# A fused attention and MLP kernel: one DMA per output tile, score pairs placed by estimated queues, the last tile in three pieces, and a new order of the first batch

## Chip, cores and metric

The kernel runs on one core of a Trainium2 chip. The metric is the device time of one execution in microseconds (us). The profile comes from one separate, profiled execution.

## What is computed

For each of 8 batches: attention over 12 heads of 448 tokens with 64 features, then a mixer of rank 32 over the tokens, then an MLP with 768 to 3072 to 768 features, both with a residual.

```python
q_n, k_n = rmsnorm(q, g_q), rmsnorm(k, g_k)            # q, k, v: (8, 12, 448, 64) float32
attn = softmax(q_n @ k_n^T / sqrt(64))
x = (attn @ v), heads side by side                     # (8, 448, 768)
u = x + (x^T @ U @ V)^T                                # U (448, 32), V (32, 448): over the tokens
out = u + relu(u @ w_ch1) @ w_ch2                      # (768, 3072), (3072, 768); float32
```

## The kernel before

**Tiles.** Matmuls are in bf16. The 448 tokens of a batch stand as three and a half windows of 128; the half window (column SM = 384) is shared by two consecutive batches, which share the tiles uT (u transposed, the input of the MLP) and hT (its hidden layer). Four heads are a *group*, a group has two *pairs* of heads, a batch has three groups and six pairs. Score and product blocks are in PSUM tiles from two pools (`ps_sc`, two tiles of two banks, and `ps`, four of one bank); E (the exps of a pair) has two buffers, x three, the output tile ob three.

**One group's way.** SP loads q, k and v (`load_qk` L92, `load_v` L105). `squares` (L135) on ACT or POOL and `sums` (L161, two DVE reductions of 128x896) give the sums of squares, `roots` (L165, two small ACT instructions) the factors, `scale` (L173) the normed q and k, `values` (L199) the bf16 copy of v. In groups 0 to 5, PE transposes q and k (`turn` L349; `take_q` and `take_k`, L357 and L366, copy them from PSUM on DVE); from group 6 on, SP issues transposing DMAs (`turn_dma`, L375 to L381) and POOL multiplies the gains in (`take_dma`, L386).

**Attention.** In the first batches scores are made by `Sc` (L403: block r of a pair, exp at L416 on ACT), later by `Spair` (L421), which makes all seven score matmul groups of a pair and their exps in one go: its matmuls are at L427, L436 and L438. `V(pair, half)` (L450) multiplies E with the values (matmuls L462 and L466) and normalizes on DVE (L469, L470) into x.

**Mixer.** In the first batch `mix_t0` (L496) makes a piece of tz = x^T U, and `mix` (L506) adds V's product to x's transpose and writes uT. Later batches use `mix_t` (L480: 24 matmuls, the DVE copy tb at L487), `mix_tr` (L489: two transposes of tb, a DVE copy tT) and `mix_rows` (L526: eight pieces; matmul L537, the residual on DVE at L542, a transposing DMA to uT at L548).

**MLP.** `up(b, ht)` (L550) makes one of 24 row blocks of the hidden layer (6 matmuls of 448 columns at L554, relu on ACT at L561 or on DVE); `down` (L579) makes a half (384 columns) of an output tile in four quarters of 6 matmuls (L586), adds u on DVE (L596), and issues two DMAs per tile, one of 64 partitions each (L604). `w1` and `w2` are loaded in chunks by POOL (`weights`).

**What sets the order.** The engines execute in the order in which the program issues, and each engine's queue is in order. Ahead of the loop the first group is made by hand. The first batch's attention follows the table `extra` (L632 to L656): what is issued behind score block (pair, r), with `keep_busy` (L237: blocks of 4 small matmuls that write nothing that is used). Everything else is in two lists, `att` (attention of batches 1 to 7) and `mlp` (mixer and MLP). The loop at L854 merges them: by their estimated costs it takes an attention item when `due` says so and `ready` (L845) allows it, else an MLP item. `at` holds an estimated end of the queue of PE, ACT and DVE, which `runs(engine, us)` advances in the functions. `ready` lets a pair (`Spair`) start except directly behind a mixer item:

```python
if f is Spair:
    return im == 0 or not mixes(mlp[im - 1][1])
```

Of the kernel before, what the change touches and what calls it, by code (L numbers as in the profile page):

```python
# [9 lines left out]
FP32 = mybir.dt.float32  # L10
# [3 lines left out]
ALU = AluOpType  # L14
# [12 lines left out]
def kernel(  # L27
# [13 lines left out]
    nc = tc.nc  # L41
# [75 lines left out]
    def stage_tiles(gi):  # L117
        staged[gi] = [stage.tile([P, NM + 2, D], FP32, name=nm, tag=nm) for nm in ("qf", "kf", "vf")]
        ssqs[gi] = normp.tile([P, 2, NM + 2], FP32, name="ssq", tag="ssq")
        normed[gi] = [normp.tile([P, NT, 2, D], BF16, name="qn", tag="qn", bufs=1)]  # L120
        if gi < DMA_FROM:
            normed[gi].append(kp[:, :NT].rearrange("p j (c d) -> p j c d", c=2))
        else:
            normed[gi].append(kp)
        normed[gi] += [va_bufs[gi % 3], vl_bufs[gi % 3]]
# [73 lines left out]
    def values(gi):  # L199
        tv, va, vl = staged[gi][2], *normed[gi][2:]  # L200
        nc.gpsimd.tensor_copy(va[:, :, :D], tv[:, :NM, :])
        for e in range(2):
            nc.gpsimd.tensor_copy(vl[e * R:(e + 1) * R, :, e * D1:e * D1 + D], tv[e * R:(e + 1) * R, NM:, :])
# [93 lines left out]
    Urows = moe_U.rearrange("(p j) r -> p j r", j=NT)  # L297

    def load_u():
        for i in range(2):  # L300
            nc.sync.dma_start(Uf[i * R:(i + 1) * R, :NJ, :], Urows[:, i * NJ:(i + 1) * NJ, :])
        nc.sync.dma_start(Uf[R:P, NJ, :], Urows[:, 2 * NJ, :])
        nc.sync.dma_start(Uf[0:R, NJ + 1, :], Urows[:, 2 * NJ, :])
        nc.sync.dma_start(Vf, moe_V.rearrange("(m r) s -> m r s", m=1).to_broadcast([NQ, rank, S]))
# [175 lines left out]
    def mix_t(b):  # L480

        pt = ps.tile([P, KD, rank], FP32, name="pu", tag="ps")
        for dt in range(KD):
            for j in range(NW):
                nc.tensor.matmul(pt[:, dt, :], xs[b][:, j, dt * P:(dt + 1) * P], Ub[:, j if j < NJ else NJ + b % 2, :],  # L485
                                 start=(j == 0), stop=(j == NW - 1))
        nc.vector.tensor_copy(tb_bufs[b % 2][:, :KD * rank], pt.rearrange("p k r -> p (k r)"))  # L487

    def mix_tr(b):  # L489
        pt = ps.tile([P, 2, P], BF16, name="pw", tag="ps")  # L490
        for i in range(2):
            nc.tensor.transpose(pt[:, i, :], tb_bufs[b % 2][:, i * P:(i + 1) * P], ident)
        tTs[b] = headp.tile([P, 2, P], BF16, name="tT", tag="tT")
        nc.vector.tensor_copy(tTs[b], pt)

    def mix_t0(lo, hi, scalar=False):  # L496

# [78 lines left out]

    down_ps, down_sb = {}, {}

    def down(b, col, half, part, nparts):  # L579
        key = (b, col, half)  # L580
        if part == 0:
            down_ps[key] = ps.tile([P, HALF], FP32, name="po", tag="ps")
        po = down_ps[key]
        n = KH // nparts
        for ht in range(part * n, (part + 1) * n):
            nc.tensor.matmul(po, hT[:, ht, col:col + P], w2b[:, ht, half * HALF:(half + 1) * HALF],  # L586
                             start=(ht == 0), stop=(ht == KH - 1))
        runs("pe", 0.98)
        if part < nparts - 1:
            return  # L590
        runs("dve", 0.55)
        h = slice(half * HALF, (half + 1) * HALF)
        if half == 0 or b == 0:
            down_sb[(b, col)] = outp.tile([P, dm], FP32, name="ob", tag="ob")
        ob = down_sb[(b, col)]
        nc.vector.tensor_tensor(ob[:, h], po, urows(b, col, half), ALU.add)  # L596
        if half == 1 or b == 0:
            h = h if b == 0 else slice(0, dm)

            def rows(b, j):  # L600
                return out[b].rearrange("(p j) d -> j p d", j=NT)[j]
            for i in range(2):
                o = rows(b, i * NJ + col // P) if col != SM else rows(b - i, 2 * NJ)
                nc.sync.dma_start(o[:, h], ob[i * R:(i + 1) * R, h])  # L604


    pairs = [(b, pr) for b in range(B) for pr in range(NPAIR)]
# [13 lines left out]
    def V2(i, half):  # L621
        return (0.55, V, (*pairs[i], half))

    pool = nc.gpsimd

    def scales(gi):
        return [(0, roots, (gi,)), (0, scale, (gi, 0, pool)), (0, scale, (gi, 1, pool))]

    def turns(gi):
        return [(0.4, turn, (gi, 0)), (0, take_q, (gi, 0)), (0, take_q, (gi, 1)), (0.4, turn, (gi, 1)), (0, take_k, (gi, 0))]  # L630

    extra = {  # L632
        (0, 0): [(0, keep_busy, (8,))],
        (0, 1): [(0, keep_busy, (8,))],
        (0, 2): scales(1) + [(0, squares, (2, 1, pool)), (0, keep_busy, (8,))],
        (0, 3): [(0, keep_busy, (8,))],
        (1, 0): [(0, keep_busy, (8,))],
        (1, 1): [V2(0, 0), (0, keep_busy, (6,))],
        (1, 2): [(0.4, turn, (1, 0)), (0, take_q, (1, 0)), (0, take_q, (1, 1)), (0, keep_busy, (8,))],
        (1, 3): [(0.4, turn, (1, 1)), (0, take_k, (1, 0)), V2(0, 1), (0, take_k, (1, 1)), (0, sums, (2, 1)),  # L640
                 (0, values, (1,)), (0, load, (4,)), (0, weights, (1,))],
        (2, 1): scales(2) + [(0, weights, (1,)), V2(1, 0)],
        (2, 2): [(0, keep_busy, (6,))],
        (2, 3): [V2(1, 1), (0, prep_u, ())],
        (3, 0): [(0, keep_busy, (6,))],
        (3, 1): [V2(2, 0)],
        (3, 2): turns(2),
        (3, 3): [V2(2, 1), (0, take_k, (2, 1)), (0, squares, (3, 0, pool)), (0, values, (2,)), (0, load, (5,)),
                 (0, weights, (1,)), (0, prep_v, (0, 1)), (0, squares, (3, 1, pool)), (0, weights, (1,))],
        (4, 0): [V2(3, 0)],  # L650
        (4, 1): [V2(3, 1), (0, sums, (3, 0))],
        (5, 0): [(0.9, mix_t0, (0, 512))],
        (5, 1): [V2(4, 0)],
        (5, 2): [V2(4, 1), (0.39, mix, (0, 0))],
        (5, 3): [(0.39, mix, (0, 1)), (0.2, mix_t0, (512, 640)), (0, prep_v, (1, NQ)), (0, weights, (2,))],
    }  # L656
    for i in range(NPAIR):
        for r in range(4):
            add_att(0.38, Sc, *pairs[i], r)
            att.extend(extra.get((i, r), []))  # L660
    att.extend([V2(5, 0), V2(5, 1), (0, sums, (3, 1)), (0.39, mix, (0, 2, True)), (0.39, mix, (0, 3, True)), (0.57, up_part, (0, 0, 0, 3)),
                (0.2, mix_t0, (640, dm)), (0.39, mix, (0, 4, True)), (0, roots, (3,)), (0.57, up_part, (0, 1, 0, 3)),
                (0.39, mix, (0, 5)), (0.19, up_part, (0, 0, 3, 4)), (0.19, up_part, (0, 1, 3, 4))])
    first_done = len(att)

# [87 lines left out]
    for b in range(B):  # L753
        for ht in range(KH):
            mlp.append((0.38, up_part, (b, ht, 4, KD), b) if b == 0 and ht < 2 else (1.14, up, (b, ht), b))
            if b < ROWS_FROM and ht % 2 == 0 and ht < 4 * NW:
                mlp.append((0.17, mix_rows, (b, ht // 4, ht // 2 % 2), b))
        cols = (64, 192, 320) if b % 2 == 0 else (384, 0, 128, 256)
        n = len(cols) * 8
        nb = b + 1  # L760
        pre = {}
        if ROWS_FROM <= nb < B:
            pre[n - PRE[nb > 1]] = [(0.77, mix_t, (nb,), nb)]
            pre[n - PRE[nb > 1] + 1] = [(0.11, mix_tr, (nb,), nb)]
            for piece in range(2 * NW):
                pre.setdefault(n - PRE[nb > 1] + 2 + (piece if nb > 1 else piece // 2), []).append(
                    (0.17, mix_rows, (nb, *divmod(piece, 2)), nb))
        tiles = [(col, half) for col in cols for half in range(2)]
        if b == 0:
            tiles.sort(key=lambda t: t[1])  # L770
        for c, (col, half) in enumerate(tiles):
            for part in range(4):
                mlp.extend(pre.get(c * 4 + part, []))
                mlp.append((0.98, down, (b, col, half, part, 4), b))

    a_, b_ = PARTS
    squares_part(0, *a_)
# [13 lines left out]
    for part in PARTS:  # L791
# [3 lines left out]
    fill_mixer()  # L795
    squares(2, 0, nc.gpsimd,
            uT.rearrange("p k c -> p (k c)")[:, :4 * NT * D].bitcast(FP32).rearrange("p (j d) -> p j d", d=D))
    values(0)
    turn(0, 0)
    keep_busy(14)  # L800
    take_q(0, 0, True)
# [5 lines left out]
    sums(1, 1)  # L807
    take_k(0, 1)
    sums(2, 0)
    stage_tiles(3)  # L810
    load_u()
    load_v(2)
    load_qk(3, 0)
    load_qk(3, 1)
    load_v(3)

    ia = im = 0
    ca = cm = 0.0
# [23 lines left out]
    def mixes(f):  # L842
        return f in (mix_t, mix_tr, mix_rows)

    def ready(f, a):  # L845
        if f is Spair:
            return im == 0 or not mixes(mlp[im - 1][1])
        if ca >= a_one:
            return True
        if f is V:  # L850
            return exp_done[a[:2]] <= at["pe"] + 0.1
        return f is not Srows or at["act"] <= at["pe"] + 0.6
# [69 lines left out]
```

## Time and profile before

| | us |
|---|---|
| median of 3 runs | 586.98 (586.29 to 587.7) |
| the profiled execution, its own time | 586.64 |
| its span, first to last instruction | 584.8 |
| PE busy / ACT / POOL / DVE | 572.2 / 307.9 / 210.3 / 196.8 |
| mean granted PE clock | 0.999 of full speed |

The span is what the profile sees, and the profiled execution's own time includes 1.84 us around it. A row such as `L596 DVE TENSOR_TENSOR ob<-po,x 128x384 f32<-128x384 f32 x1` names the line, engine, operation, the tile written and those read, and the shapes; brackets hold the idle time before it and what ended that. A row of PE's waits gives what PE waited for, in us in total, times, and the longest. By the view of windows PE is busy 17.4 of the first 20.0 us, 18.8 of the next 21.3, 276.2 of the 278.7 us up to 320, 259.9 of the 260 up to 580, and none of the last 4.8 us.

### The profile page before, as it was taken

The page shows a single profiled execution, that of the slowest core. Times are in us where ns is not written, and L with a number is a line of the kernel's source. Part 1 is how long each engine was busy: PE and PEld are TensorE (multiplying, and loading weights), DVE is VectorE, ACT ScalarE, POOL GpSimd, SP SyncE. Part 2 cuts the span into 40 slices and gives each one's busy share as a digit, 9 for nine tenths or more (in the row PEclk, how much of TensorE's full clock was granted, in tenths as well). Part 3 has the DMA queues.
Part 4 walks back from the last instruction along what each step waited for, and adds up shares of the span by engine and source line. Part 5 has one row for each costly group of instructions (what it writes and reads, how often), then busy time and mean ns, then how long its engine had stood idle before and what let it go on. Part 6 is the DMA issues. An engine that isn't in the chain of part 4 may idle for free.

```text
span 584.8 us, 11725 instructions
## 1 busy us (share of the span) xinstructions
PE 572.2 (98%) x4826; PEld 338.2 (58%) x4826; DVE 196.8 (34%) x458; ACT 307.9 (53%) x510; POOL 210.3 (36%) x310
## 2 busy tenths in 40 slices
PE   8899999999999999999999999999999999999996
PEld 7555556555665555655556555665556655655563
DVE  6676656212352232521235231442034310410011
ACT  7866661677445776277653578457753344014200
POOL 5995684265314515334523433441531000000000
PEclk9999999999999999999999999999999999999999
DMA  8899999683546642585246735375204210420022
GB/s 229 170 241 241 244 233 231 119 220 52 133 78 167 153 106 35 139 212 130 36 122 109 180 104 123 66 172 149 35 25 92 48 28 1 68 61 1 1 54 55
DMA packets 104509, 68.21 MB, mean 117 GB/s; under 512 B 66568, under 2 KB 101256, under 8 KB 104456
## 3 DMA queue, kind: packets, MB, share of 16 engines
q1 hardware_dynamic: 95044, 58.03, 42.6%
q0 software_dynamic: 9408, 9.44, 9.6%
q8 instruction: 38, 0.62, 0.4%
q14 instruction: 15, 0.12, 0.1%
q10 hardware_dynamic: 4, 0.00, 0.0%
HBM read 52.20 MB, written 11.01 MB: 108 GB/s over the span
## 4 chain that ended last, share of the span: by engine, by line
PE 91%; DMA 3%; DVE 2%; POOL 1%; ACT 1%; issue 1%; SPq 1%; POOLq 0%; ACTq 0%
PE ph L554 36%; PE po L586 36%; PE pv L466 6%; PE sc L436 2%; PE sl L427 2%; PE sl L438 2%; PE pv L462 2%; PE pm L537 2%; DMA qf<-in_q_dram 1%; PE sc L415 1%; ACT E L416 1%; DMA vf<-in_v_dram 1%; DVE ssq L162 1%; DMA qT<-qn 1%; PE pu L485 1%
## 5 line engine op out<-in xcount | busy, mean ns | idle before, releaser
L586 PE MATMUL po<-w2b,hT 128*128 128x384 bf16 x1344 | 237.4, 326 | 0.0
L554 PE MATMUL ph<-uT,w1b 128*128 128x448 bf16 x1140 | 228.7, 352 | 0.0
L586 PEld LDWEIGHTS <-hT 128*128 128x128 bf16 x1344 | 126.8, 98 | 75.5 <-issue 0.6
L554 PEld LDWEIGHTS <-w1b 128*128 128x128 bf16 x1140 | 108.3, 98 | 93.8 <-issue 0.7
L561 ACT ACTIVATE hT<-ph 128x448 bf16<-128x448 f32 x184 | 98.0, 550 | 120.2 <-PE ph L554 118.9
L429 ACT ACTIVATE E<-sl,gg 128x448 bf16<-128x448 f32 x72 | 41.5, 629 | 75.9 <-PE sl L427 75.9
L386 POOL TENSOR_SCALAR qT<-qT,gg 128x448 bf16<-128x448 bf16 x36 | 50.5, 1402 | 81.6 <-DMA qT<-qn 65.2
L193 POOL TENSOR_TENSOR qn<-qf,rs 128x384 bf16<-128x384 f32 x36 | 29.9, 829 | 132.4 <-ACT rs L170 127.5
L469 DVE RECIPROCAL r<-pv 128x4 f32<-128x4 f32 x96 | 17.4, 182 | 167.8 <-PE pv L466 167.6
L441 ACT ACTIVATE E<-sc,gg 128x896 bf16<-128x896 f32 x72 | 69.0, 1022 | 0.0
L596 DVE TENSOR_TENSOR ob<-po,x 128x384 f32<-128x384 f32 x48 | 26.7, 557 | 103.8 <-PE po L586 103.4
L466 PE MATMUL pv<-va,E 128*128 128x65 bf16 x1152 | 57.1, 194 | 0.0
L466 PEld LDWEIGHTS <-E 128*128 128x128 bf16 x1152 | 50.5, 98 | 6.3
L162 DVE TENSOR_REDUCE ssq<-sq 128x14 f32<-128x896 f32 x45 | 46.8, 1078 | 2.4 <-ACT sq L140 2.3
L462 PE MATMUL pv<-vl,E 128*128 128x130 bf16 x192 | 42.2, 220 | 0.3 <-ACT E L416 0.2
L470 DVE TENSOR_TENSOR x<-pv,r 128x256 bf16<-128x256 f32 x96 | 40.7, 424 | 3.3
L416 ACT ACTIVATE E<-sc,gg 128x896 bf16<-128x896 f32 (+1 forms) x42 | 37.5, 950 | 4.1 <-PE sc L415 4.1
L542 DVE TENSOR_TENSOR x<-pm,x 128x384 bf16<-128x384 f32 x48 | 26.2, 552 | 16.5 <-PE pm L537 14.2
L193 POOL TENSOR_TENSOR kp<-kf,rs 128x384 bf16<-128x384 f32 x36 | 29.8, 828 | 0.0
L169 ACT ACTIVATE rs<-ssq,eps 128x28 f32<-128x28 f32 (+1 forms) x25 | 7.8, 314 | 33.4 <-DVE ssq L162 29.2
L462 PEld LDWEIGHTS <-E 128*128 128x128 bf16 x192 | 18.7, 97 | 9.7 <-issue 2.0
L439 ACT ACTIVATE E<-sl,gg 128x448 bf16<-128x448 f32 x36 | 22.9, 637 | 0.0
(102 smaller groups left out, 387.9 us busy)
## 6 DMA issues: line engine op xcount, KB each, us to landing
qf<-in_q_dram SPq DMA_DIRECT2D x23, 448.0 KB, 3.7
kf<-in_k_dram SPq DMA_DIRECT2D x23, 448.0 KB, 6.4
out_dram<-ob SPq DMA_DIRECT2D x50, 192.0 KB, 2.8
vf<-in_v_dram SPq DMA_DIRECT2D x48, 192.0 KB, 5.9
w1b<-in_moe_w_ch_dram POOLq DMA_DIRECT2D x4, 1152.0 KB, 19.8
w2b<-in_moe_w_ch_dram POOLq DMA_DIRECT2D x8, 576.0 KB, 17.7
vf<-in_v_dram SPq DMA_DIRECT2D x48, 32.0 KB, 5.7
out_dram<-ob SPq DMA_DIRECT2D x12, 96.0 KB, 3.6
```

The costliest lines, as they stand in the source:

```text
L162: nc.vector.tensor_reduce(ssqs[gi][:, i, :], sqs.pop((gi, i)), AX, ALU.add)
L193: nc.gpsimd.tensor_tensor(main.rearrange("p (t i) d -> p i t d", i=2), src[:, c, :2 * NJ].rearrange("p (i t) d -> p i t d", i=2), rs[:, c, ...
L386: nc.gpsimd.tensor_scalar(qT[:, a], qT[:, a], gg[:, 0:1], None, ALU.mult)
L416: nc.scalar.activation(es[(b, pr)][:, 2 * r:2 * r + n, :], sc[:, :n, :S], AF.Exp, scale=scal, bias=bias)
L429: nc.scalar.activation(E[:, 4 + i, :], ts[i], AF.Exp, scale=scal, bias=bias)
L441: nc.scalar.activation(E[:, 2 * r:2 * r + 2, :], tiles[r][:, :, :S], AF.Exp, scale=scal, bias=bias)
L462: nc.tensor.matmul(pv[:, i].rearrange("p e d -> p (e d)"), E[:, 2 * NJ, w:w + P], vl[:, lp, :], start=True, stop=False)
L466: nc.tensor.matmul(pv[:, i, e, :], E[:, 2 * j + e, w:w + P], va[:, (first_h + step * e) * NJ + j, :], start=False, stop=(e == 1 and j == N ...
L470: nc.vector.tensor_tensor(xs[b].rearrange("p i (h d) -> p i h d", d=D)[:, 2 * half:2 * half + 2, h0:h0 + step + 1:step, :], pv[:, :, :, :D ...
L554: nc.tensor.matmul(ph, w1b[:, dt, ht * P:(ht + 1) * P], uT[:, dt, off:off + S], start=(dt == 0), stop=(dt == KD - 1))
L561: nc.scalar.activation(hT[:, ht, off:off + S], ph, AF.Relu)
L586: nc.tensor.matmul(po, hT[:, ht, col:col + P], w2b[:, ht, half * HALF:(half + 1) * HALF], start=(ht == 0), stop=(ht == KH - 1))
```

## The change

One. The stores: a new function `store` issues one DMA for an output tile, with an access pattern over both token halves; the tile of column SM keeps two, as its halves belong to two batches. The first two of U's loads become one.

Two. `mix_t` and `mix_tr` now advance the estimated queues of PE and DVE, and a pair may start only where the estimated queues of DVE and ACT are not too far ahead of PE's.

Three. The last output tile (batch 7, column 256) is made in pieces of 384, 256 and 128 columns by `down_end`, each with an add and a DMA of its own.

Four. The first batch: group 1 is scaled behind score block (0, 1) instead of (0, 2); the cast of group 0's values follows it on POOL; SP's loads for group 3 go ahead of U, V and the values (`front_loads`); the products V of pair 0 move behind block (2, 0); group 1's turns go one block earlier; group 2 is scaled behind (2, 2) instead of (2, 1); `prep_u` follows values(2); the mixer's first product, 512 columns at once behind (5, 0), becomes two of 256 behind (5, 0) and (5, 2), and `mix(0, 0)` moves to (5, 3).

```diff
     def load_u():
-        for i in range(2):
-            nc.sync.dma_start(Uf[i * R:(i + 1) * R, :NJ, :], Urows[:, i * NJ:(i + 1) * NJ, :])
+        nc.sync.dma_start(Uf[:, :NJ, :], Urows[:, :2 * NJ, :].rearrange("p (i j) r -> i p j r", i=2))
...
         nc.vector.tensor_copy(tb_bufs[b % 2][:, :KD * rank], pt.rearrange("p k r -> p (k r)"))
+        runs("pe", 0.62)
+        runs("dve", 0.35)
...
         nc.vector.tensor_copy(tTs[b], pt)
+        runs("pe", 0.11)
+        runs("dve", 0.3)
...
+    def store(b, col, h, ob):
+        def rows(b):
+            return out[b].rearrange("(p j) d -> j p d", j=NT)
+        if col == SM:
+            for i in range(2):
+                nc.sync.dma_start(rows(b - i)[2 * NJ, :, h], ob[i * R:(i + 1) * R, h])
+        else:
+            nc.sync.dma_start(rows(b)[col // P:col // P + NJ + 1:NJ, :, h], ob[:, h])
+
+    ENDS = (HALF, 5 * P, dm)
+
+    def down_end(b, col, piece):
+        lo, hi = (0, HALF) if piece == 0 else ENDS[piece - 1:piece + 1]
+        if piece == 0:
+            down_sb[(b, col)] = outp.tile([P, dm], FP32, name="ob", tag="ob")
+        ob = down_sb[(b, col)]
+        po = ps.tile([P, HALF], FP32, name="po", tag="ps")[:, :hi - lo]
+        for ht in range(KH):
+            nc.tensor.matmul(po, hT[:, ht, col:col + P], w2b[:, ht, lo:hi], start=(ht == 0), stop=(ht == KH - 1))
+        nc.vector.tensor_tensor(ob[:, lo:hi], po, xs[b][:, col // P, lo:hi], ALU.add)
+        store(b, col, slice(lo, hi), ob)
...
-            def rows(b, j):
-                return out[b].rearrange("(p j) d -> j p d", j=NT)[j]
-            for i in range(2):
-                o = rows(b, i * NJ + col // P) if col != SM else rows(b - i, 2 * NJ)
-                nc.sync.dma_start(o[:, h], ob[i * R:(i + 1) * R, h])
+            store(b, col, h, ob)
...
+    def front_loads():
+        stage_tiles(3)
+        load_qk(3, 0)
+        load_qk(3, 1)
+        load_u()
+        load_v(2)
+        load_v(3)
...
         (0, 0): [(0, keep_busy, (8,))],
-        (0, 1): [(0, keep_busy, (8,))],
-        (0, 2): scales(1) + [(0, squares, (2, 1, pool)), (0, keep_busy, (8,))],
+        (0, 1): scales(1) + [(0, values, (0,)), (0, front_loads, ()), (0, squares, (2, 1, pool)), (0, weights, (1,)),
+                             (0, keep_busy, (8,))],
+        (0, 2): [(0, keep_busy, (8,))],
...
-        (1, 1): [V2(0, 0), (0, keep_busy, (6,))],
-        (1, 2): [(0.4, turn, (1, 0)), (0, take_q, (1, 0)), (0, take_q, (1, 1)), (0, keep_busy, (8,))],
-        (1, 3): [(0.4, turn, (1, 1)), (0, take_k, (1, 0)), V2(0, 1), (0, take_k, (1, 1)), (0, sums, (2, 1)),
-                 (0, values, (1,)), (0, load, (4,)), (0, weights, (1,))],
-        (2, 1): scales(2) + [(0, weights, (1,)), V2(1, 0)],
-        (2, 2): [(0, keep_busy, (6,))],
-        (2, 3): [V2(1, 1), (0, prep_u, ())],
+        (1, 1): [(0.4, turn, (1, 0)), (0, take_q, (1, 0)), (0, take_q, (1, 1)), (0, keep_busy, (6,))],
+        (1, 2): [(0, keep_busy, (8,))],
+        (1, 3): [(0.4, turn, (1, 1)), (0, take_k, (1, 0)), (0, keep_busy, (4,))],
+        (2, 0): [V2(0, 0), V2(0, 1), (0, sums, (2, 1)), (0, take_k, (1, 1)), (0, values, (1,)), (0, load, (4,))],
+        (2, 1): [V2(1, 0)],
+        (2, 2): scales(2) + [(0, weights, (1,)), (0, keep_busy, (6,))],
+        (2, 3): [V2(1, 1), (0, squares, (3, 0, pool))],
...
-        (3, 2): turns(2),
-        (3, 3): [V2(2, 1), (0, take_k, (2, 1)), (0, squares, (3, 0, pool)), (0, values, (2,)), (0, load, (5,)),
-                 (0, weights, (1,)), (0, prep_v, (0, 1)), (0, squares, (3, 1, pool)), (0, weights, (1,))],
+        (3, 2): [(0.4, turn, (2, 0)), (0, take_q, (2, 0)), (0, take_q, (2, 1))],
+        (3, 3): [(0.4, turn, (2, 1)), (0, take_k, (2, 0)), V2(2, 1), (0, take_k, (2, 1)), (0, values, (2,)), (0, load, (5,)),
+                 (0, prep_u, ()), (0, weights, (1,)), (0, prep_v, (0, 1)), (0, squares, (3, 1, pool)), (0, weights, (1,))],
...
-        (5, 0): [(0.9, mix_t0, (0, 512))],
+        (5, 0): [(0.45, mix_t0, (0, 256))],
         (5, 1): [V2(4, 0)],
-        (5, 2): [V2(4, 1), (0.39, mix, (0, 0))],
-        (5, 3): [(0.39, mix, (0, 1)), (0.2, mix_t0, (512, 640)), (0, prep_v, (1, NQ)), (0, weights, (2,))],
+        (5, 2): [V2(4, 1), (0.45, mix_t0, (256, 512))],
+        (5, 3): [(0.39, mix, (0, 0)), (0.39, mix, (0, 1)), (0.2, mix_t0, (512, 640)), (0, prep_v, (1, NQ)), (0, weights, (2,))],
...
-    values(0)
...
-    stage_tiles(3)
-    load_u()
-    load_v(2)
-    load_qk(3, 0)
-    load_qk(3, 1)
-    load_v(3)
...
         if f is Spair:
-            return im == 0 or not mixes(mlp[im - 1][1])
+            if im > 0 and mixes(mlp[im - 1][1]):
+                return False
+            return at["dve"] <= at["pe"] + 0.3 and at["act"] <= at["pe"] + 1.0
```

In the last batch the `mlp` list drops the two halves of the last tile and gets three `down_end` items of 3.9, 2.6 and 1.3 us of estimated cost instead. `sums(3, 1)` moves behind `mix_t0(640, 768)`.

More of the change, by code (lines that the diff above doesn't have):

```diff
@@ L660 @@
             att.extend(extra.get((i, r), []))
-    att.extend([V2(5, 0), V2(5, 1), (0, sums, (3, 1)), (0.39, mix, (0, 2, True)), (0.39, mix, (0, 3, True)), (0.57, up_part, (0, 0, 0, 3)),
-                (0.2, mix_t0, (640, dm)), (0.39, mix, (0, 4, True)), (0, roots, (3,)), (0.57, up_part, (0, 1, 0, 3)),
+    att.extend([V2(5, 0), V2(5, 1), (0.39, mix, (0, 2, True)), (0.39, mix, (0, 3, True)), (0.57, up_part, (0, 0, 0, 3)),
+                (0.2, mix_t0, (640, dm)), (0, sums, (3, 1)), (0.39, mix, (0, 4, True)), (0, roots, (3,)), (0.57, up_part, (0, 1, 0, 3)),
                 (0.39, mix, (0, 5)), (0.19, up_part, (0, 0, 3, 4)), (0.19, up_part, (0, 1, 3, 4))])
@@ L770 @@
             tiles.sort(key=lambda t: t[1])
+        if b == B - 1:
+            tiles = tiles[:-2]
         for c, (col, half) in enumerate(tiles):
@@ L774 @@
                 mlp.append((0.98, down, (b, col, half, part, 4), b))
+    mlp.extend((3.9 * w, down_end, (B - 1, cols[-1], piece), B - 1) for piece, w in enumerate((1.0, 0.67, 0.34)))
     a_, b_ = PARTS
```

## Prediction

> **What bounds the kernel now.** I read the page's busy times first.
>
> ```profile
> PE 572.2 (98%) x4826; PEld 338.2 (58%) x4826; DVE 196.8 (34%) x458; ACT 307.9 (53%) x510; POOL 210.3 (36%) x310
> PEclk9999999999999999999999999999999999999999
> ```
>
> PE is busy 572 of 584.8 us at full clock, so only PE's idle time, the head and the tail can give anything: nothing in the change shortens a matmul stream. Next the list of PE's waits (line waited for: us in total, times, longest):
>
> ```profile
> PE sc L415 <- ACT E L416: 2.1, 4, 0.9
> ...
> PE sl L427 <- POOL qT L386: 1.1, 1, 1.1
> PE sl L438 <- DVE tb L487: 0.6, 1, 0.6
> PE sl L427 <- DVE x L542: 0.5, 1, 0.5
> PE sc L415 <- DVE kT L369: 0.5, 1, 0.5
> ```
>
> The rows with L427 and L438 are score pairs that meet a wait after 41 us. In front of 41 us PE is fed keep_busy blocks and ACT's exps set the pace. I looked for each row in the timelines and added the PE start-to-start distances above normal: 1.15 us at 115.72 (a pair waits for POOL's qT), 0.88 at 175.66 and 0.36 at 239.32 (pairs wait for a PSUM buffer that DVE's L542 holds), 0.72 at 303.98 (waits for tb's copy), 0.39 and 0.19 elsewhere: 3.7 us after 41 us.
>
> **1. Scores by estimated queues.** A pair may now start only where DVE's estimated queue ends at most 0.3 us, and ACT's 1.0 us, after PE's. The order of the instructions shows which move. All else on PE keeps its sequence, so a moved pair's stall either vanishes or appears elsewhere.
>
> At 115.7 the pair goes behind one more `up` (6 x 189 ns = 1.13 us). Its qT also comes sooner, as SP's queue says:
>
> ```profile
> 105.88 1.22 SPq L548 DMA_TRANSPOSE uT<-u_rest  x1
> 107.19 2.46 SPq L604 DMA_DIRECT2D out_dram<-ob  x4
> 109.76 1.56 SPq L378 DMA_TRANSPOSE qT<-qn  x1
> ```
>
> Two of four stores go (one DMA per tile), and the transposes stand earlier in SP's order. Stall gone: **-1.15**. If the up did not move but the stores did, 2.46/2 = 1.23 would still cover it.
>
> At 174.8 the pair's second matmul waits for a buffer whose reader stands on DVE behind two sums:
>
> ```profile
> 174.08 1.07 DVE L162 TENSOR_REDUCE ssq<-sq 128x14 f32<-128x896 f32 x1
> 175.07 0.55 DVE L542 TENSOR_TENSOR x<-pm,x 128x384 bf16<-128x384 f32 x1
> ```
>
> In the new order it follows the last mix_rows and two quarters of a down tile (2 x 0.97 us), longer than the 0.88 it waits: **-0.88**. At 239 it goes behind two more mix_rows: **-0.36**. What those leave on DVE is two L542 (1.1 us), with a spare PSUM buffer.
>
> At 302.6 the pair moves behind mix_tr and mix_rows, so its 0.72 goes, but mix_tr is now one down quarter behind mix_t and needs tb, whose copy stands on DVE so:
>
> ```profile
> 301.12 0.56 DVE L596 TENSOR_TENSOR ob<-po,x 128x384 f32<-128x384 f32 x1 [1.31 <-PE po L586]
> 301.60 2.07 DVE L162 TENSOR_REDUCE ssq<-sq 128x14 f32<-128x896 f32 x2
> 303.58 0.35 DVE L487 CAST tb<-pu 128x192 bf16<-128x192 f32 x1
> ```
>
> DVE's order here is unchanged: tb ends at 303.93. Today the pair (302.59 to 303.33) fills most of that time; without it PE runs dry at about 302.50. This adds a wait: behind mix_tr on PE stand mix_rows, the pair and all the rest, and nothing passes it. So 303.98 - 302.50 = 1.48 instead of 0.72: **+0.76**. The estimates now charge mix_t and mix_tr, but not the sums in front of them, so they do not see it.
>
> Sum: -1.15 - 0.88 - 0.36 + 0.76 = **-1.63**. Bounds: -3.1 if tb is early (all four stalls gone), +0.8 if only the new wait arrives and the moved pairs each meet a wait as long as their old one. I take the sum: each term is from a row at the same place.
>
> **2. The last tile in three** (384, 256, 128 columns, not 384 and 384). PE: adds of consecutive halves start 3.90 us apart, so a 384-column matmul takes 162 ns; 128-column matmuls with a weight load each go at 56 ns in the chain of waits (L512: 0.17 us for three), 256 lies between at 109. 24 x (162 + 109 + 56) = 7.85 us against 7.78: +0.07. *The Trainium skill (TensorE: Matmul & The Clock Gate, Back-to-back issue gap) says that a sustained stream of weight load and matmul pairs at 128 columns goes at about 81 ns each, which speaks against the split; by that page the piece would cost 24 x 25 ns = 0.6 us more and the total would come out that much later. The trace's 56 ns are of short runs of three only; no row has 24.* I take 56.
>
> Behind the last matmul (579.86) today:
>
> ```profile
> 579.88 0.56 DVE L596 TENSOR_TENSOR ob<-po,x 128x384 f32<-128x384 f32 x1 [3.34 <-PE po L586]
> 580.47 1.11 SPq L604 DMA_DIRECT2D out_dram<-ob  x2
> ```
>
> with the DMA view of that window:
>
> ```profile
> out_dram<-ob SPq DMA_DIRECT2D x2, 192.0 KB, 2.6
> ```
>
> The second is issued at 580.98 and lands at 583.6; the span ends 1.17 us later. Afterwards: the add has 128 columns, 0.29 us (a 128x128 copy from PSUM, L504, takes 285 ns, V's 256 columns 424); one issue at once, so 0.51 us of queueing go; 64 KB land in 2.0 to 2.6 us (8 KB of U 2.0, 24 KB 2.3, 192 KB 2.6; I take 2.3, as the middle piece's 128 KB are still moving). 0.02 + 0.29 + 0.03 + 2.3 + 1.17 = 3.8 against 4.94. The end gains 1.13 - 0.07: **-1.06**. Bounds: -1.4 (2.0 us to land) and +0.2 (2.6 us, and a distance of 98 ns, what one weight load of L586 takes, so 24 x 42 ns = 1.0 more).
>
> **3. One DMA per tile.** 62 stores (50 of 192 KB, 12 of 96 KB) become 37, and U's two first loads one; each that goes frees about 0.55 us of SP's issue time. That is worth something only where PE waits for what SP issues, and in the list of waits this is the one row with POOL qT (counted above): **0**. A store of 384 KB is not in the trace: 448 KB of q land in 3.7 us, 192 KB of output in 2.8, so ob would be held at most 1 us longer; a tile takes 7.8 us and there are three buffers, so nothing comes to wait (if it did, DVE's one wait on out_dram, 0.2 us, is the nearest row).
>
> **4. First batch.** POOL's chain has scale(1) (1.69 us for each of q and k), values(0) (1.41), then squares(2). Now values(0) comes after scale(1), which comes after roots(1), themselves after the second exp instead of the third: roots end near 14.2, scale(1) spans 14.3 to 17.6, values(0) ends at 19.0, as against 15.6 before. kT is ready at 18.65 where it was 20.1, and the big gap on ACT seems to go:
>
> ```profile
> 18.63 0.64 ACT L416 ACTIVATE E<-sc,gg 128x448 bf16<-128x448 f32 x1 [0.49 <-PE sc L415]
> 20.52 1.90 ACT L416 ACTIVATE E<-sc,gg 128x896 bf16<-128x896 f32 x2 [1.26 <-PE sc L415]
> ```
>
> But it is filled only in part: the exp of pair 2 writes one of two E buffers, so it waits for V(0,0) and V(0,1), which wait for values(0) at 19.0; two V of 0.5 us and the last latency put it at 20.3, a gain of 0.2. Then even that is lost: roots(2) moves from behind block (2,1) to (2,2), scale(2) runs 23.6 to 27.0 instead of 23.4 to 26.7, and pair 4's first exp, which needs it, starts at about 28.45 instead of 28.42. So up to pair 4: **0**. From there mix_t0's split (4 matmuls of 512 columns, 0.97 us on PE in front of block (5,1)) removes ACT's 0.20 and 0.16 us gaps at 32.95 and 35.02, and the mixer's first column goes behind the exps: block (5,3) ends at 35.2 instead of 35.65: **-0.35**. Bounds: -1.75 (the 1.26 and 0.49 gaps truly gone), +0.6 (scale(2) 0.3 late and prep_u, which now ends at 31.5 just in front of mix_t0's start at 31.6, 0.3 late too). I take the chain, as every link has a row. w1's chunks are requested no later, and DMA has room between 16 and 20 us; the cover of this zero is that w1's first chunk landed at 36.46 and is first used at 37.5.
>
> **Sum.** -1.63 - 1.06 + 0 - 0.35 = -3.04 from the profiled 586.64 (span 584.8 and 1.84 around it): 583.60. The median of the three runs, 586.98, is 0.34 above that execution; by it the sum is 583.94. I take the middle: **583.8 us**. What this kernel's measurement can tell from no change is 0.2%, 585.8 to 588.15.
>
> **Rivals.**
> - *The head gains its gaps* (ACT starts pair 2 at once): 583.8 - 1.4 = 582.4. For: kT is 1.45 us earlier. Against: two E buffers. 0.13.
> - *The middle gives nothing*: each moved pair meets another wait. 583.8 + 1.6 = 585.4. For: the +1.48 above shows how. Against: the other places have idle DVE behind them. 0.15.
> - *The rule for pairs does not move what it should, and the head eats the tail*: all gains under 1.2 us, 586.2. 0.08.
> - *Slower: values(0) becomes the head's bound.* Behind scale(1) it now also waits for roots(1) on ACT; if V(0,\*) are late, E's buffers block the exps, squares(2,1), values(1), scale(2), turn(2) and prep_u follow on POOL, and mix_t0, in order on PE, blocks block (5,1). A us that reaches the exps is a us of the head, and no later stage gives it back. values(0) ends 3.4 us later than today; if all of it arrived, with one exp (1.0) that roots(1) may wait for, the head would be 4.4 longer instead of 0.35 shorter: 583.8 + 0.35 + 4.4 = 588.5. It decides from 4.0 us on. Against: the exp of pair 2 has 1.26 us of gap today to absorb it, and POOL is idle 0.43 us ahead of scale(2). 0.06.
> - *Forecast*: 0.58, its own range 582.7 to 584.8.
>
> Faster by over 0.2%: 0.58 + 0.13 + 0.15 = 0.86, less 0.01: 0.85; within: 0.08 + 0.01 = 0.09; slower: 0.06. Leaving out most of the slower case and half of the third, the range is 581.9 to 586.0.
>
> **What would show it.** Right: the list of PE's waits loses L427 <- POOL qT and L427 <- DVE x, and gains about 1.5 us of pw on tb's copy near 302; ACT's exp of pair 2 at 20.3; the last DVE add of 128 columns in 0.29 us and 3.8 us from the last matmul to the span's end; first whole `up` near 40.9. Wrong: an exp of pair 2 near 19, 24 last matmuls taking over 1.7 us, a pair waiting elsewhere.

## The result, and the profile after

The changed kernel takes 614.46 us (609.69 to 615.89), the kernel before 586.85: a ratio of 1.046, with a 95% interval of 1.0424 to 1.0496. The forecast was 583.8 in a range of 581.9 to 586.0. The profiled execution took 615.89 us, its span is 613.8.

The page of the changed kernel, busy times, granted clock and chain:

```profile
PE 578.7 (94%) x4858; PEld 341.9 (56%) x4858; DVE 196.7 (32%) x460; ACT 309.2 (50%) x510; POOL 209.8 (34%) x310
PEclk9999999879999899998999999999999999999996
PE 82%; DMA 9%; SPq 3%; ACT 1%; POOL 1%; DVE 1%; issue 1%; POOLq 0%; DVEq 0%; ACTq 0%
```

PE now idles 35 us instead of 13, DMA has 9% of the chain instead of 3%, and the granted clock, unbroken before, has dips. PE's list of waits (line waited for: us in total, times, longest):

```profile
PE sl L426 <- POOL qT L385: 11.3, 3, 6.1
PE sl L437 <- DVE ob L621: 2.6, 1, 2.6
...
PE pw L493 <- DVE tb L486: 1.3, 1, 1.3
...
PE ph L557 <- DMA uT<-u_rest: 0.8, 1, 0.8
```

The wait on POOL's qT was to vanish; it grew tenfold. POOL is not what is late: ahead of the longest of the three waits it is idle for 19.75 us, until the transposing DMA has landed.

```profile
126.24 2.78 POOL L385 TENSOR_SCALAR qT<-qT,gg 128x448 bf16<-128x448 bf16 x2 [19.75 <-DMA qT<-qn]
```

SP's own queue ahead of it (start, duration), and last the same three transposes in the kernel before:

```profile
102.59 1.36 SPq L589 DMA_DIRECT2D out_dram<-ob  x2
104.06 9.60 SPq L551 DMA_TRANSPOSE uT<-x  x3
113.75 1.21 SPq L551 DMA_TRANSPOSE uT<-u_rest  x1
115.06 1.12 SPq L589 DMA_DIRECT2D out_dram<-ob  x2
116.28 4.00 SPq L377 DMA_TRANSPOSE qT<-qn  x1
```

```profile
101.36 4.44 SPq L548 DMA_TRANSPOSE uT<-x  x3
```

Directly behind two merged stores, three transposes that took 4.44 us to issue take 9.60, and those of q and k follow late. They also land late. At each of the three waits the chain of work goes through a transpose of q that SP issues directly behind a merged store, and it takes some 10 us from issue to landing (start, duration; the one at this place in the kernel before took 4.32):

```profile
116.28 9.77 DMA qT<-qn
198.15 10.72 DMA qT<-qn
266.39 10.44 DMA qT<-qn
```

The DMA view shows what the second of them waits for. From 205 to 207.4 us only the store's packets of 3 KB move (first line); the transposes' small packets, under 512 B, come in mass from 207.9 to 209 us (second line):

```profile
DMA packets 41, 0.13 MB, mean 52 GB/s; under 512 B 0, under 2 KB 0, under 8 KB 41
DMA packets 945, 0.23 MB, mean 210 GB/s; under 512 B 945, under 2 KB 945, under 8 KB 945
```

The end of the kernel shows the merged stores alone (the issue of the four last ones, and the last add):

```profile
593.63 11.48 SPq L589 DMA_DIRECT2D out_dram<-ob  x4
...
600.90 0.29 DVE L601 TENSOR_TENSOR ob<-po,x 128x128 f32<-128x128 f32 x1 [0.91 <-PE po L600]
```

From the last matmul (600.87) to the span's end pass 12.9 us, where 3.8 were forecast and 4.94 were there before. The view of windows says what moves in that time; the last three columns are the granted clock, the mean busy share of the 16 DMA engines and GB/s. First the changed kernel, then the kernel before while its last two stores move:

```profile
602.00:610.00 8.00, 0.00 (x0) 0.00 (x0) 0.00 (x0) 0.00 (x0) 0.00 (x0) 0.56 0.13 50
```

```profile
581.00:583.70 2.70, 0.00 (x0) 0.00 (x0) 0.00 (x0) 0.00 (x0) 0.00 (x0) 0.96 0.56 146
```

A share of 0.13 held for 8 us is 2 of 16 engines (0.125), at 25 GB/s each. The merged store's access pattern in the output is 2 x 64 rows: its outer dimension is 2. A whole tile of 384 KB so takes some 8 us, where the two DMAs before took about 3.

### The profile page after: what moved, and what is told of

The parts are those of the page before. It is cut to its first block, busy times and chain, and to the rows that moved or that the text cites. A ratio compares the mean times of both kernels' runs of the same rounds, so it can differ in the third digit from the quotient of the medians.

```text
span 613.8 us, 11772 instructions
## 1 busy us (share of the span) xinstructions
PE 578.7 (94%) x4858; PEld 341.9 (56%) x4858; DVE 196.7 (32%) x460; ACT 309.2 (50%) x510; POOL 209.8 (34%) x310
## 4 chain that ended last, share of the span: by engine, by line
PE 82%; DMA 9%; SPq 3%; ACT 1%; POOL 1%; DVE 1%; issue 1%; POOLq 0%; DVEq 0%; ACTq 0%
PE ph L557 33%; PE po L611 30%; PE pv L465 5%; DMA qT<-qn 5%; DMA vf<-in_v_dram 2%; PE sc L435 2%; PE sl L426 2%; PE sl L437 2%; PE pv L461 2%; PE pm L540 1%; PE po L600 1%; DMA qf<-in_q_dram 1%; DMA out_dram<-ob 1%; SPq L110 1%; PE sc L414 1%; ACT E L415 1%
## 5 line engine op out<-in xcount | busy, mean ns | idle before, releaser
L557 PE MATMUL ph<-uT,w1b 128*128 128x448 bf16 x1140 | 231.9, 356 | 0.8 <-DMA uT<-u_rest 0.8
L611 PE MATMUL po<-w2b,hT 128*128 128x384 bf16 x1296 | 231.0, 327 | 0.0
L611 PEld LDWEIGHTS <-hT 128*128 128x128 bf16 x1296 | 122.5, 98 | 75.2 <-issue 3.8
L465 PEld LDWEIGHTS <-E 128*128 128x128 bf16 x1152 | 50.9, 98 | 6.3
L426 PE MATMUL sl<-qT,kT 64*128 64x448 bf16 x72 | 13.5, 371 | 11.3 <-POOL qT L385 11.3
## 6 DMA issues: line engine op xcount, KB each, us to landing
w2b<-in_moe_w_ch_dram POOLq DMA_DIRECT2D x8, 576.0 KB, 16.6
```

The source lines that it names most:

```text
L465: nc.tensor.matmul(pv[:, i, e, :], E[:, 2 * j + e, w:w + P], va[:, (first_h + step * e) * NJ + j, :], start=False, stop=(e == 1 and j == N ...
L557: nc.tensor.matmul(ph, w1b[:, dt, ht * P:(ht + 1) * P], uT[:, dt, off:off + S], start=(dt == 0), stop=(dt == KD - 1))
```

## The experiments

Each kernel was timed against runs of the kernel before on the same chip, whose medians were 586.59 (e1 to e4), 586.19 (e5, e6, e7 and e12) and 586.15 us (e8, e9 and e10). As these differ by up to 0.4 us for one and the same kernel, differences of that size across the groups say little.

| run | us | what it is |
|---|---|---|
| e1_two_stores | 584.45 | the change, with two stores per tile and U's load in two |
| e2_one_store | 621.24 | before, with merged stores |
| e3_128_rows | 583.87 | the change, merged store with an outer dimension of 128 |
| e4_split_by_columns | 610.67 | before, two stores per tile, each with an outer dimension of 2 |
| e9_outer_4, e10_outer_8 | 594.47, 584.46 | merged stores with an outer dimension of 4 and 8 |
| e5_old_head | 583.53 | e1 with the old first batch |
| e6_old_rule | 584.75 | e1 with the old pair rule |
| e7_three_pieces | 585.08 | before, with the last tile in three |
| e12_scale2_early | 583.50 | e1, group 2 scaled behind (2, 1) |
| e8_mended | 581.76 | e12, mix_tr later, last stores from two queues |

**e1: the change without the merge.**

```diff
-            nc.sync.dma_start(rows(b)[col // P:col // P + NJ + 1:NJ, :, h], ob[:, h])
...
+        for i in range(2):
+            o = rows(b, i * NJ + col // P) if col != SM else rows(b - i, 2 * NJ)
+            nc.sync.dma_start(o[:, h], ob[i * R:(i + 1) * R, h])
```

> The changed kernel, with two DMAs of 64 rows per output tile again and U's first load in two; pieces, pair rule and first batch stay changed. Theory (a merged store, whose outer dimension in DRAM is 2, moves on two of the 16 DMA engines at some 46 GB/s and holds up the transposes behind it): the three waits on POOL qT (11.3 us) and the 13 us behind the last matmul go, and the time is what the rest of the change was forecast to give, 583 to 585. Rival (the rule for pairs or the new first batch make the waits): the time stays above 600. Third (many bytes in one DMA are slow, whatever its form): also 583 to 585 here; the run with stores split by columns tells it apart.

584.45 us, ratio 0.9963 (0.9945 to 0.9981) to before: 0.4% faster than before, and 30.0 us of the change's time are gone with one edit. The span falls from 613.8 to 582.4, 31.4 us, and the two traces say where they were. From the first whole `up` to the last matmul 558.98 us pass in the changed kernel and 536.99 in e1, 22.0 less; the stretch behind the last matmul shrinks by 9.1, from 12.9 to 3.8. Of PE's waits this is left after 100 us:

```profile
PE pw L494 <- DVE tb L487: 1.3, 1, 1.3
```

The pair rule and the first batch do not make the waits. Whether it is the form of the store or its size, e1 can't tell.

**e2 and e4: the merge alone, and its form without its size.** e2 puts the merged stores and U's merged load into the kernel before. e4 keeps two DMAs per tile, but cuts them by columns:

```diff
+            mid = (h.start + h.stop) // 2
+            for c in (slice(h.start, mid), slice(mid, h.stop)):
+                nc.sync.dma_start(rows(b)[col // P:col // P + NJ + 1:NJ, :, c], ob[:, c])
```

> The kernel before, with only the stores and U's load merged. Theory: most of the loss is here, 600 to 620, with an end of about 13 us behind the last matmul and waits on POOL qT. Rival (pair rule, first batch): within 2 us of the kernel before.

> The kernel before, with two DMAs per tile as ever, but each over both halves of the rows (outer dimension 2) and half of the columns (1.5 KB rows, 0.75 KB in the first batch). Theory: as slow as one merged store or slower, 600 to 620, though the number of DMAs and the bytes in each are those of before. Rival (one large DMA per tile is the trouble): 586 to 588.

e2 takes 621.24 us (ratio 1.0588, 1.0539 to 1.0637), slightly above what was expected, e4 610.67 (1.0412, 1.0394 to 1.0429). Two of PE's waits in e4 and its end, where the last stores move alone:

```profile
PE sl L427 <- POOL qT L386: 8.6, 3, 6.8
PE po L597 <- DVE ob L607: 4.3, 1, 4.3
```

```profile
603.00:607.00 4.00, 0.00 (x0) 0.00 (x0) 0.00 (x0) 0.00 (x0) 0.00 (x0) 0.57 0.13 48
```

The count and the bytes of e4's DMAs are those of before, and the same waits and the same share of 0.13 are there. So neither size nor number is the cause; and as e4 loads U in two, U's merged load isn't needed for the loss.

**e3, e9, e10: the outer dimension as the dose.** In these the rows of each batch stand in another order in the output than the reference's, chosen so that one tile's 128 rows are 128 at one step, or 4 x 32, or 8 x 16; the bytes and the rows of 3 KB stay the same. U's load is in two. The main lines of e9, where e10 has e=28 and 8 * NJ:

```diff
...
-            nc.sync.dma_start(rows(b)[col // P:col // P + NJ + 1:NJ, :, h], ob[:, h])
+            rows = out[b].rearrange("(p e) d -> e p d", e=14)
+            nc.sync.dma_start(rows[col // P:4 * NJ:NJ, :, h], ob[:, h])
```

> The changed kernel, with U's load in two, and one DMA per tile, but into rows of the output that are one dimension of 128 at equal steps of three rows (and the shared half window into the last 64 rows of its batch), so that the rows of each batch stand in another order than the reference's. Same bytes, same 3 KB rows, same number of DMAs. Theory (the outer dimension of 2 confines the DMA): time as with two stores, 583 to 585, DMA share at the end near 1. Rival (one large DMA behind which others queue is slow whatever its form): as the changed kernel, above 605.

> One DMA per tile as in the changed kernel, U's load in two, but the rows of the output are taken so that the outer dimension is 4 and the inner one 32 (the rows of a batch stand in another order than the reference's; all are written). Theory (as many DMA engines work as the outer dimension counts): DMA share at the end 4/16 = 0.25, some 95 GB/s, 384 KB in about 4 us instead of 8; most waits go, time 584 to 592. Rival (any outer dimension under 16 falls back to two engines): as the changed kernel, above 605.

> The same with an outer dimension of 8 and an inner one of 16 (rows in another order than the reference's). Theory: DMA share 0.5 and some 190 GB/s where a store is alone, time 583.5 to 585, close to the one of 128. Rival as for 4: above 605.

583.87, 594.47 and 584.46 us, for outer dimensions of 128, 4 and 8, beside 614.46 for 2. PE's waits for POOL's qT go the same way: 6.3 us for 4 and none for 8 and 128, beside 11.3 for 2. e9's time is above its range of 584 to 592, its share and rate are as expected (two windows near its end):

```profile
584.00:587.00 3.00, 2.78 (x38) 2.47 (x35) 0.60 (x2) 0.00 (x0) 0.00 (x0) 1.00 0.25 94
587.00:590.00 3.00, 0.00 (x0) 0.00 (x0) 0.11 (x1) 0.00 (x0) 0.00 (x0) 1.00 0.27 96
```

Twice the share and nearly twice the rate of outer dimension 2. For 8 the store is over too soon for a long flat stretch; one of half a microsecond reads 0.50 and 190 GB/s, as expected:

```profile
577.20:577.70 0.50, 0.50 (x13) 0.50 (x11) 0.43 (x1) 0.00 (x0) 0.00 (x0) 1.00 0.50 190
```

In e3, with 128, a merged store lands quickly; the share near 1 that was expected at its end holds only for some 0.4 us (0.8 to 0.9), as 128 KB are gone by then:

```profile
out_dram<-ob SPq DMA_DIRECT2D x20, 384.0 KB, 3.2
out_dram<-ob SPq DMA_DIRECT2D x15, 192.0 KB, 3.4
```

384 KB in 3.2 us, where the two halves of 192 KB took 2.8 each. So the forecast's figure for one store per tile was right for a form that the change doesn't have. The Trainium skill (DMA: Bandwidth & Descriptors, Rules for kernel authors) says that a DMA uses at most as many engines as the slowest dimension of its access patterns counts, where that is under 16; shares of 0.13, 0.25 and 0.50 agree. Another row of that list of the Trainium skill advises one 128-partition transfer instead of two to disjoint partition halves; here that holds in e3 (583.87 us against 584.45 in e1) and is wrong in the changed kernel (614.46), so the measurement decides, by the form.

**e5, e12: the first batch.** e5 is e1 with the old table and the old start; e12 moves one entry of e1's table:

```diff
-        (2, 1): [V2(1, 0)],
-        (2, 2): scales(2) + [(0, weights, (1,)), (0, keep_busy, (6,))],
+        (2, 1): scales(2) + [V2(1, 0)],
+        (2, 2): [(0, weights, (1,)), (0, keep_busy, (6,))],
```

> The kernel with two stores per tile, the new pair rule and the last tile in three, but the first batch (and U's load) in its old order. Theory from the traces (the new first batch takes 30.24 us from its first score block to the first whole up, the old one 29.4 to 30.0): 0.2 to 0.8 us faster than e1, so 583.6 to 584.2. Rival (the forecast, the new order gains 0.35): 0.3 slower than e1, 584.8.

> e1 with group 2's roots and scales back behind score block (2, 1), the rest of the new first batch as it is. Theory (the new first batch loses where scale(2) starts 0.8 us later on POOL, which sets the exp of pair 4): pair 4's first exp comes about 0.8 us sooner and the time is 583.6 to 583.8. Rival (it loses at pair 2's exp, which waits for E's buffer, and nothing later matters): as e1, 584.4.

583.53 and 583.50, both about 0.9 less than e1 (0.5 less, if each is taken against the kernel before in its own group). POOL's first scale of group 2 and pair 4's first exp on ACT, first in e1, then in e12:

```profile
24.17 1.68 POOL L174 TENSOR_TENSOR qn<-qf,rs 128x896 bf16<-128x896 f32 x1 [0.82 <-POOL vl L203]
```

```profile
29.04 6.86 ACT L416 ACTIVATE E<-sc,gg 128x896 bf16<-128x896 f32 x8 [1.27 <-PE sc L415]
```

```profile
23.41 1.68 POOL L174 TENSOR_TENSOR qn<-qf,rs 128x896 bf16<-128x896 f32 x1
```

```profile
28.28 1.91 ACT L416 ACTIVATE E<-sc,gg 128x896 bf16<-128x896 f32 x2 [0.49 <-PE sc L415]
```

The scale starts 0.76 us sooner, the exp 0.76, and the first whole up is at 40.86 instead of 41.63. That late scale is all that the new first batch loses; with it mended the rest of the new order brings nothing over the old (40.97 in e5).

**e6, e7: the pair rule and the last tile.** e6 takes the rule and the estimates out of e1; e7 puts only `down_end` (two stores per piece) into the kernel before.

> e1 (two stores, new first batch, last tile in three) with the old pair rule and without the estimates in mix_t and mix_tr. Theory: the four stalls of before at 116, 175, 239 and 304 us come back and the one of 1.5 us at mix_tr goes, so e1 + 1.6, about 586. Rival (the pair rule is worth nothing once the tile's stores are two): as e1, 584.4.

> The kernel before with only the last tile in pieces of 384, 256 and 128 columns, two stores each. Theory: 3.8 us instead of 4.94 behind the last matmul and 0.07 more on PE, so 1.1 less than before: 585.5. Rival (a sustained stream of 128-column matmuls at 81 ns, or six small stores queueing on SP): within 0.5 of before.

e7: 585.08 us, 1.1 less than before (ratio 0.9987, 0.9971 to 1.0003, which doesn't exclude zero), with 3.8 us behind the last matmul in the trace, as expected. e6: 584.75, only 0.3 more than e1 (0.7 against the kernel before in their groups) where 1.6 were expected, a miss. Its trace has the four stalls, at 116, 176, 239 and 304 us, together 2.6 us against 1.5 for the one in e1 at 302; but that profiled execution is, with 585.42, the slowest of e6's 11. The stall at 116 depends on when a transpose lands (0.65 us in e6's trace, 0.94 in e7's, 1.15 in before's), and may be gone in the faster ones. So the rule is worth 0.3 to 0.7 in the times; why it is not the 1.2 of the two spans stays open.

**e8: mended.** e12, and in the list of MLP items `mix_tr` with all `mix_rows` two down quarters later, and the second half-store of the last pieces issued by ACT:

```diff
-            pre[n - PRE[nb > 1] + 1] = [(0.11, mix_tr, (nb,), nb)]
+            gap = 3 if nb > 1 else 1
+            pre[n - PRE[nb > 1] + gap] = [(0.11, mix_tr, (nb,), nb)]
...
+            eng = nc.scalar if i and b == B - 1 and h != slice(0, dm) else nc.sync
+            eng.dma_start(o[:, h], ob[i * R:(i + 1) * R, h])
```

> The best parts together: e12 (two stores per tile, new pair rule, last tile in three, group 2 scaled early) with mix_tr and the mix_rows behind it two down quarters later in the list of batches 2 and on, and the second half-store of the last three pieces issued by ACT. Theory: the 1.49 us wait of mix_tr on tb goes, as two quarters are 1.95 us, and the last store goes out 0.58 us sooner: e12 - 2.0, about 581.5. Rival (the later mix_rows meet another wait, or the queue of ACT issues no sooner): 583 and more.

581.76 us, ratio 0.9919 (0.9897 to 0.994): faster than both kernels. The only start-to-start distance of PE clearly above normal after 100 us that is left is one of 0.19, and from the last add's start to the span's end pass 3.4 us instead of 3.8.

## Why the prediction was wrong

**Step 3, "One DMA per tile ... 0", failed.** The forecast took the landing of a 384 KB store from rows that do not share its form: q's 448 KB load (3.7 us) has 128 partitions as one dimension in DRAM, and the two half stores have 64 rows each. From them came "ob would be held at most 1 us longer", and so no wait. The merged store has 2 x 64 rows and 2 of 16 engines: some 8 us. It cost time at three places. SP's transposes behind it came late, with them POOL's qT and the score pair (11.3 us of PE waits). Of ob's buffers one add waited 8 us for a store, and PE 2.6 us for that add. The last tiles' stores queue behind one another at the end (+9.1 us against e1). The step looked at ob's buffers alone, and from the wrong duration; of what stands behind a store on SP it counted only the issue time that is saved. No rival held this: the slower one was placed in the head, with another mechanism.

**Step 1, the pair rule: its traced stalls were right.** The stalls at 115.7, 175.7 and 239 us are gone in e1, and the new wait of `mix_tr` on tb measured 1.49 us against 1.48 forecast. The sum of -1.63 agrees with the traces (3.7 to 2.1 us); the timed runs of e6 show only 0.3 to 0.7 of it. Part of it is luck: in e5, with the new rule and the old first batch, a wait for POOL's qT of 0.61 us stands again at 116.0, so the rule alone does not make that place safe.

**Step 2, the last tile: right in its size, partly by luck.** With two stores per piece 3.8 us pass behind the last matmul, as forecast for one store. But two are still issued one behind the other, and 32 KB land in 1.9 us, where the forecast had no queueing and 2.3 us; with one store at the end, in e3, 3.2 us pass. The 128-column piece's add starts 1.34 us after the add ahead of it, so 24 matmuls go at 56 ns each. The 81 ns that the Trainium skill (TensorE: Matmul & The Clock Gate, Back-to-back issue gap) states for a sustained stream do not fit these 24.

**Step 4, the first batch: wrong sign, small size.** Forecast -0.35. In e1 30.24 us pass from the first score block to the first whole up; in the old order 30.02 in the profiled execution of before, but 29.44 to 29.47 in the traces of e2, e4, e5 and e7. So that one execution was slow at its start (POOL waited 3.06 us for a load of q, 1.15 to 2.22 in those four), and the new order is 0.8 longer than the usual old one. The term that was mis-sized is scale(2): put at +0.03 for pair 4's exp, which measured from the first score block starts at 17.66 us in e1 instead of 16.6 in those four (17.16 in the execution that the forecast read), so +1.07. The gain behind it, forecast at 0.35, came with 0.3. Pair 2's exp starts at 20.77, not at the forecast 20.3.

Without step 3 the traces of e1 and of before so give -1.6, -1.1 and +0.2 for the terms forecast at -1.63, -1.06 and -0.35. That e1 lies inside the range says nothing for the forecast of the change, whose step 3 it takes out.

## What to carry to other kernels

Before DMAs are merged, look at the slowest dimension of the access pattern on both sides (here the output's side was varied): an outer dimension of 2 makes two engines work, however many partitions the tile has. The DMA busy share of a window in which one transfer moves alone (0.13 for 2, 0.25 for 4) shows it, and one that stays flat and low is the sign to look for. When a duration is borrowed from another DMA, borrow it from one of the same form, and name all that is queued behind on the same issuing engine.

## What the runs showed of the hardware

A long stall of PE costs more than itself. In the changed kernel PE waits 6.05 us for qT at 127.69, and then the granted clock is 0.5 (third column from the end) for a while; the DMA share next to it is over 1 because packets overlap in the records:

```profile
128.00:131.40 3.40, 3.40 (x13) 1.22 (x10) 0.00 (x0) 3.03 (x5) 3.40 (x6) 0.50 1.07 315
```

A 448-column matmul starts every 373 ns there, 189 elsewhere. The trace's stretches at 0.5 in mid-kernel last 3.41 us or twice that. After stalls of 2.3, 2.7, 3.1, 3.2 (e9) and 6.1 us such a stretch came, after 1.2 and 2.0 (e9) none; in e2 and e4 it came after five stalls of 2.4 to 6.9 us, and after none of 2.1 us or less. Of the 22.0 us more between the first whole `up` and the last matmul than in e1, 15.2 are the stalls and some 7 the slow matmuls behind them.

A transpose behind a merged store lands late (9.77 to 10.72 us from issue). Why its issue takes longer too (9.60 us for three instead of 4.44), and whether merged stores from another engine's queue would let the transposes pass, no run here shows.
